# Window attention on one core: VectorE's exp in four passes instead of five, a larger share of score tiles for GpSimd, and a padded lead-in

## The chip, the cores and the metric

The kernel runs on one core of one Trainium2 chip. The metric is the device time of one execution in microseconds (us). Before the change it was 1091.46 us, the median of 3 runs (1091.45 to 1091.47).

Five engines matter here. In this kernel TensorE (PE in the profile) multiplies matrices into PSUM. ScalarE (ACT), VectorE (DVE) and GpSimd (POOL) compute element by element, and SyncE (SP) starts transfers. The other tiles that this text names are in SBUF. Each row of the profile carries a line number of the kernel file.

## The reference, cut to what matters

```
x: 1 x 224 x 224 x 96, bf16; wqkv: 96 x 288; wo: 96 x 96; stripes 8 wide
qkv = x @ wqkv; q, k, v have 96 channels each
channels 0..47:  28 horizontal stripes of 8 x 224 = 1792 tokens
channels 48..95: 28 vertical stripes of 224 x 8 = 1792 tokens
each stripe: softmax(q @ k.T / sqrt(48)) @ v
out = concat(horizontal, vertical) @ wo
```

Two stripes are handled together as one pair, so there are 28 pairs. The 1792 x 1792 scores of the two stripes of a pair are cut into 49 tiles of 128 x 1024. That makes 28 x 49 = 1372 score tiles, and each needs one exp of 131,072 elements. Getting those exponentials done is most of the work that is not on TensorE.

Of the kernel before, what the change touches and what calls it, by code (L numbers as in the profile page):

```python
# [11 lines left out]
ALU = mybir.AluOpType  # L12
# [8 lines left out]
def bass_standalone__window_attn_cswin__vision_kernel(  # L21
# [25 lines left out]
    NGTOT = NP * NG  # L47
# [3 lines left out]
    VS = 10  # L51
    NXB = 3
    NTMP = 5
    NZP = 1
    PCH = NTOK // 4
    PU = PCH // SW
    NBD = 3
    SWITCH = 100.0
    DPOL = 0
    SLACK = 120  # L60
    PACE = 1
    FDUE = 20.0
    DSLACK = 120.0
    GRP = 2
    NBA = 8
    LOOK = 8
    NPT = 400
    XPV = 3
    NBP = 3
    NRES = 0  # L70
    RDUE = 0
    KWP = 1
    KWL = 0
    HOLD = 0.0
    HOLD2 = 0
    DUEO = 18
    DUES = 2
    DUE1 = 0
    DUEV = 10
    LATE = 10  # L80
    UTH = 3
    PSPAN = 12
    SAFE = 100
    WGAP = 170
    ORD = 1
    LOOKP = 32
    WARM = 600
    NCHT = NP * NCH
    KA = C2 + 1
    KD = C2 + 2  # L90
# [11 lines left out]
    with es:  # L102
# [104 lines left out]
        def t_ps(n):  # L207
            return 1.0417 * n + 75.0
# [91 lines left out]
        rr = [0]  # L300
# [9 lines left out]
        def fill_bank():  # L310
            if startup[0]:
                rr[0] += 1
                return 4 + rr[0] % 4
            if tail[0]:
                bs = sorted((4, 5, 6, 7), key=lambda i: vis(bank_free[i]) if bank_free[i] != "busy" else 1e18)
                return bs[0]
            bi = pvb.get(pv_cur[0])
            if bi is not None:
                return 13 - bi

            return max((6, 7), key=lambda i: 1e18 if bank_free[i] == "busy" else vis(bank_free[i]))
# [419 lines left out]
        def pick_pe():  # L741
# [47 lines left out]
            if D["cur"] is None and fits(240.0, "r64", DSLACK):  # L789
                G = max(progress(), lastA[0]) + LOOK  # L790
                while G < NGTOT and taken[G] is not None:
                    G += 1
                if G < NGTOT - 6:
                    deps = tile_deps(G)
                    if deps is not None:
                        ws = list(deps) + [D.get("free")]
                        if all(vis(w) <= t for w in ws):
                            taken[G] = "d"
                            ev = plan_QK(G, 4, KD, ws)
                            D["cur"] = dict(G=G, k=0, prev=ev, qk=ev)  # L800
                            return True
# [94 lines left out]
            return True  # L896

        dps = ps[:, 4 * 512:6 * 512]
        D_OCC = [t_ps(1024), 0.521 * 1024 + 75, 0.26 * 1024 + 75, 0.521 * 1024 + 75, t_ps(1024)]

        def d_step(k, sl):
            if k == 0:
                return lambda e: e.tensor_scalar(tt_sb[:], dps.bitcast(U16)[:, 0:2048:2], CS / 65536.0, CS * CA3, ALU.mult, ALU.add)  # L903
            if k == 1:
                return lambda e: e.tensor_tensor(sq_sb[:], tt_sb[:], tt_sb[:], ALU.mult)  # L905
            if k == 2:
                return lambda e: e.tensor_scalar(sq_sb[:], sq_sb[:], CB, None, ALU.add)  # L907
            if k == 3:
                return lambda e: e.tensor_tensor(tt_sb[:], sq_sb[:], tt_sb[:], ALU.mult)  # L909
            return lambda e: e.scalar_tensor_tensor(PTD[sl][:].bitcast(U16), dps, CC, tt_sb[:], ALU.add, ALU.add)  # L910

        def pick_dve():
            t = now[0]
            if evac_pv:
                chg, bi, P, c, e_pv = evac_pv[0]
                if vis(e_pv) <= t:
                    evac_pv.pop(0)
                    q0, qs = CH_Q0[c], CH_SIZES[c]
                    b = P % 2
                    segs = [(0, qs, OT_sb[b][:, q0:q0 + qs], bank(bi)[:, 0:qs])]  # L920
                    if P == 0:

                        segs = []
                        dst4 = OT_sb[b][:].rearrange("p (bc r dw) -> p r bc dw", r=SW, dw=8)
                        o = q0
                        while o < q0 + qs:
                            r, col = divmod(o, W)
                            nr = (q0 + qs - o) // W if col == 0 else 0
                            n = nr * W if nr else min(W - col, q0 + qs - o)
                            sp = bank(bi)[:, o - q0:o - q0 + n]  # L930
                            if nr:
                                segs.append((o - q0, n, dst4[:, r:r + nr, :, :], sp.rearrange("p (r bc dw) -> p r bc dw", r=nr, dw=8)))
                            else:
                                segs.append((o - q0, n, dst4[:, r, col // 8:(col + n) // 8, :], sp.rearrange("p (bc dw) -> p bc dw", dw=8)))
                            o += n
                    for _, n, dst, sp in segs:
                        ev = add("dve", [e_pv], lambda e, dst=dst, sp=sp: e.tensor_copy(dst, sp), t_ps(n), t_ps(n) + 150.0)  # L937
                    bank_free[bi] = ev
                    ot_ev[chg] = ev
                    return True  # L940
            d = D["cur"]
            if DPOL == 1 and d is not None and d["k"] == 4 and do_d(t):
                return True
            if DPOL == 2 and d is not None and d["k"] >= 3 and do_d(t):
                return True
            if DPOL == 3 and d is not None and (d["k"] == 4 or d["k"] == 0) and do_d(t):
                return True
            if DPOL == 4 and d is not None and do_d(t):
                return True
            if DPOL == 5 and d is not None and d["k"] in (1, 2, 3) and do_d(t):  # L950
                return True
            if DPOL == 6 and d is not None and d["k"] in (1, 2, 3, 4) and do_d(t):
                return True
            for f in evac_q:
                if f.steps[f.k].get("eng", "dve") == "dve" and f.step_ready():
                    if f.do_step():
                        evac_q.remove(f)
                    return True
            if HOLD and d is not None and d["k"] in (0, 4) and not tail[0]:
                for f in evac_q:  # L960
                    if f.k > 0 and f.steps[f.k].get("eng", "dve") == "dve" and f.step_soon(HOLD):
                        return False
                if HOLD2 and pv_cur[0] < NCHT and pv_cur[0] not in pvb and evac_pv and vis(evac_pv[0][4]) <= t + HOLD2:
                    return False
            return do_d(t)
# [21 lines left out]
        def safe(dur):  # L987

            t = now[0]
            d = D["cur"]  # L990
            until = max(tfree["dve"], t)
            if d is None or "p" in d or d["k"] == 0:
                until += D_OCC[0]
            elif d["k"] == 4:
                until += D_OCC[4] + D_OCC[0]
            return t + dur <= until + SAFE

        def pick_pool():
# [51 lines left out]
        def do_d(t):  # L1050
            d = D["cur"]
            if d is not None and "p" in d:
# [5 lines left out]
                D["cur"] = None  # L1058
                pow_q.append(dict(G=d["G"], zi=zi, st=[0, 0], ev=[ev, ev], sl=None))
                return True  # L1060
            if d is not None and d["k"] in (1, 2, 3) and tfree["pool"] > t + 50.0:
                return False
            if d is not None and vis(d["prev"]) <= t:
                sl = D["n"] % NBD
                ws = [d["prev"]]
                ok = True
                if d["k"] == 4:
                    if D["n"] >= NBD:
                        if bufD_ev[sl] is None or vis(bufD_ev[sl]) > t:
                            ok = False  # L1070
                        ws.append(bufD_ev[sl])
                    ws.append(d["qk"])
                if ok:
# [1 line left out]
                    ev = add("dve", ws, d_step(k, sl), D_OCC[k], D_OCC[k] + 107.0)  # L1075
                    d["prev"] = ev
                    d["k"] += 1
                    if k == 4:
                        pe_t = (ev[0], ev[1], ev[2] + 28.0)
                        pt_ev[d["G"]] = (pe_t, PTD[sl], ("d", sl))  # L1080
                        bufD_ev[sl] = None
# [7 lines left out]
        pf0 = prep_fills(0, first=True)  # L1089
        def pad(n):  # L1090
            for _ in range(n):
                add("pe", [e_warm], lambda e: e.matmul(bank(3)[:, :], lhsT=warm[:, 0:128], rhs=warm[:, :], start=True, stop=True), 216.0)

        pf0["K"][0].run_now()
        pf0["Q"][0].run_now()
# [1 line left out]
        for G in range(2):  # L1097
# [2 lines left out]
            qA.append((G, plan_QK(G, 2 * G, KA, tile_deps(G))))  # L1100
            if G == 0:
                pad(0)
        for f in [pf0["K"][1], pf0["V"][0]]:
            f.run_now()

        now[0] = max(vis(ev) for _, ev in qA)
        pick_act()
        now[0] = 0.0

        def early_qk(G):  # L1110
            taken[G] = "a"
            lastA[0] = G
            qA.append((G, plan_QK(G, 2 * (G % 2), KA, tile_deps(G) + [actA[G - 2]])))
        early_qk(2)
        for f in [pf0["V"][1], pf0["K"][2]]:
            f.run_now()
        now[0] = tfree["act"]
        pick_act()
        now[0] = 0.0
        early_qk(3)  # L1120
        for f in [pf0["V"][2], pf0["K"][3]]:
            f.run_now()
        startup[0] = False
        add("dve", [bank_free[4], bank_free[5]], lambda e: e.memset(scr[:, 0:1], 0.0), 60.0)
        D["free"] = (s_dve, cnt["dve"], tfree["dve"] + 60.0)
# [173 lines left out]
```

## The kernel before: the parts that the change touches

The kernel file is a small scheduler. It keeps a model of when each engine becomes free, and from this model it decides, while the program is built, in which order each engine gets its instructions and which engine gets which score tile. The order is then fixed. If an instruction takes longer on the chip than the model thinks, nothing is rearranged, and what waits for it is late. This matters for the whole of this study.

A score tile goes to one of three engines. ScalarE has a true exp. VectorE builds the bits of a bf16 number directly: a cubic in the low 16 bits of the fp32 score corrects the score, and the integer that results is the bit pattern of the exponential. GpSimd does the same in six passes, after VectorE has copied the tile from PSUM to SBUF for it (`zp_sb`).

VectorE's five passes (`dps` is the tile in PSUM, all other operands are in SBUF) and the durations that the model gives them (the means in the profile of before were 1221, 716, 432, 696 and 1219 ns):

```python
D_OCC = [t_ps(1024), 0.521 * 1024 + 75, 0.26 * 1024 + 75, 0.521 * 1024 + 75, t_ps(1024)]

def d_step(k, sl):
    if k == 0:
        return lambda e: e.tensor_scalar(tt_sb[:], dps.bitcast(U16)[:, 0:2048:2], CS / 65536.0, CS * CA3, ALU.mult, ALU.add)
    if k == 1:
        return lambda e: e.tensor_tensor(sq_sb[:], tt_sb[:], tt_sb[:], ALU.mult)
    if k == 2:
        return lambda e: e.tensor_scalar(sq_sb[:], sq_sb[:], CB, None, ALU.add)
    if k == 3:
        return lambda e: e.tensor_tensor(tt_sb[:], sq_sb[:], tt_sb[:], ALU.mult)
    return lambda e: e.scalar_tensor_tensor(PTD[sl][:].bitcast(U16), dps, CC, tt_sb[:], ALU.add, ALU.add)
```

The scheduler is built on the assumption that some passes of VectorE and the instructions of GpSimd hold each other up. The recorded texts call what they contend for "the port"; the traces show only which instructions get longer, not what is behind it. In the trace of before, the square (L905) took 675 to 695 ns where no GpSimd instruction ran during it (126 cases) and up to 1121 where one did (32), the addition behind it (L907) 410 to 429 (143) and up to 724 (15), and the last pass (L910), which reads PSUM and one SBUF tile, 1194 to 1226 with one and 1204 to 1225 without (an overlap under 20 ns is not counted). The scheduler treats passes 1, 2 and 3 as passes to be kept apart from GpSimd's work. It does not start one of them while its model says that GpSimd is busy, and it lets GpSimd start an instruction only if that instruction ends before the next such pass can begin:

```python
def safe(dur):                       # may GpSimd start something that lasts dur?
    ...
    until = max(tfree["dve"], t)
    if d is None or "p" in d or d["k"] == 0:
        until += D_OCC[0]
    elif d["k"] == 4:
        until += D_OCC[4] + D_OCC[0]
    return t + dur <= until + SAFE
...
    if d is not None and d["k"] in (1, 2, 3) and tfree["pool"] > t + 50.0:   # in do_d: VectorE waits
        return False
```

One further pass of VectorE works on SBUF alone all through the kernel and is held back by no such rule (there are also a sum of one column per pair, and the last three final additions). It runs once per pair, 28 times in all, and shifts a part of K. In the trace of before it took 317 to 353 ns in the 23 cases without a GpSimd instruction during it, and 946 to 972 in the 5 with one:

```python
def ev2(e, bk):
    return e.tensor_scalar(KT_sb[b][:, q0:q0 + qs], KT_sb[b][:, q0:q0 + qs], shift[b][:, 0:1], None, ALU.add)
```

## Time and profile before

| | before |
|---|---|
| time | 1091.46 us |
| tiles on ScalarE / VectorE / GpSimd | 1169 / 158 / 45 |
| busy ScalarE / VectorE / GpSimd | 1077.2 / 1047.4 / 584.6 us |
| ScalarE's idle ahead of its tiles | 5.9 us |
| mean granted TensorE clock | 0.993 |

All rows but the first are from the profiled run, and that run took 1096.08 us, 4.6 us more than the median. Of the 28 runs of this kernel in the rounds of the experiments, 14 show a mean clock of 0.999 and took 1091.24 to 1092.15 us, as the median run did. The profiled run spent 13.7 us near its start at half clock, which alone takes 0.6% off the mean clock. So the runs at 0.999 did not have this dip.

The prediction below shows and reads the groups and the stages. Two more lines of the page are needed for the comparison: the granted TensorE clock in 40 equal slices (a digit is tenths of full speed, 9 is 90% or more), and the chain of work that ended last, by engine.

```profile
PEclk7999999999999999999999999999999999999999
...
ACT 71%; DVE 21%; PE 4%; POOL 1%; issue 1%; DMA 0%; SPq 0%; DVEq 0%; POOLq 0%
```

The clock is at 90% or more except in the first slice, and 71% of the last chain are ScalarE's. That is what a kernel bound by ScalarE looks like.

### The profile page before, as it was taken

How to read it: one execution, taken by the hardware profiler on the slowest of the kernel's cores; microseconds unless marked ns; L12 is line 12 of the kernel's file. 1: busy time of each engine (PE TensorE's matmuls, PEld its weight loads, DVE VectorE, ACT ScalarE, POOL GpSimd, SP SyncE). 2: the span in 40 equal slices, each digit the busy share in tenths (PEclk: the TensorE clock that was granted, in tenths of full speed). 3: DMA queues.
4: the chain of work that ended last, by engine and by line, in shares of the span. 5: the costliest groups of instructions: out<-in, count | busy, mean ns of one | idle time of the engine just before them, and what ended most of it. 6: DMA issues, size and time to landing. Idle time of an engine off the chain costs nothing.

```text
span 1094.3 us, 28704 instructions
## 1 busy us (share of the span) xinstructions
PE 1040.7 (95%) x12104; PEld 372.7 (34%) x12104; DVE 1047.4 (96%) x1712; ACT 1077.2 (98%) x1172; POOL 584.6 (53%) x451
## 2 busy tenths in 40 slices
PE   9999999999999999999999999999999999999997
PEld 2333333332333333233333333333333333333332
DVE  5999999999999999999999999999999999999996
ACT  6999999999999999999999999999999999999997
POOL 0544555453545645364564465656565565656563
PEclk7999999999999999999999999999999999999999
DMA  5301001101110120110111122122222222221111
GB/s 99 69 9 35 19 18 36 36 10 27 36 27 10 35 36 7 30 35 17 20 35 27 35 44 41 39 41 42 41 41 40 39 42 41 39 41 38 24 28 37
DMA packets 169001, 37.37 MB, mean 34 GB/s; under 512 B 168872, under 2 KB 168872, under 8 KB 168872
## 3 DMA queue, kind: packets, MB, share of 16 engines
q1 hardware_dynamic: 167256, 35.35, 17.3%
q8 instruction: 94, 1.54, 0.6%
q10 hardware_dynamic: 1616, 0.18, 0.1%
q14 instruction: 35, 0.29, 0.1%
HBM read 0.15 MB, written 9.63 MB: 9 GB/s over the span
## 4 chain that ended last, share of the span: by engine, by line
ACT 71%; DVE 21%; PE 4%; POOL 1%; issue 1%; DMA 0%; SPq 0%; DVEq 0%; POOLq 0%
ACT PTA L892 71%; DVE tt_sb L903 4%; DVE PTD L910 3%; DVE sq_sb L905 2%; DVE tt_sb L909 2%; PE ps L194 2%; PE ps L853 1%; DVE sq_sb L907 1%; DVE KT_sb L522 1%; DVE zp_sb L1056 1%; DVE tmp L624 1%; DVE OT_sb L937 1%; DVE V_sb L431 1%; POOL PTP L985 1%; DVE QT_sb L498 1%
## 5 line engine op out<-in xcount | busy, mean ns | idle before, releaser
L892 ACT ACTIVATE PTA<-ps 128x1024 bf16<-128x1024 f32 x1169 | 1075.0, 1214 | 5.9 <-PE ps L194 5.1
L194 PE MATMUL ps<-QT_sb,KT_sb 49*64 49x512 bf16 (+3 forms) x5488 | 486.5, 369 | 38.9 <-ACT PTA L892 25.5
L853 PE MATMUL ps<-PTA,V_sb 128*64 128x512 bf16 (+1 forms) x2674 | 422.9, 367 | 0.6 <-DVE Ph_sb L584 0.2
L190 PEld LDWEIGHTS <-KT_sb 49*64 49x64 bf16 (+1 forms) x5488 | 137.4, 103 | 335.0 <-issue 321.9
L903 DVE TENSOR_SCALAR tt_sb<-ps 128x1024 f16<-128x1024 uint16 x158 | 192.9, 1221 | 11.6 <-PE ps L194 7.1
L910 DVE SCALAR_TENSOR_TENSOR PTD<-ps,tt_sb 128x1024 uint16<-128x1024 f32 x158 | 192.5, 1219 | 1.3
L853 PEld LDWEIGHTS ps<-PTA,V_sb 128*64 128x64 bf16 x2674 | 119.8, 108 | 204.1 <-issue 162.8
L647 POOL TENSOR_TENSOR out_sb<-tmp,Ph_sb 128x480 bf16<-128x480 f32 (+2 forms) x89 | 105.6, 1195 | 110.9 <-DVE sq_sb L907 57.9
L978 POOL TENSOR_TENSOR uq_sb<-up_sb 128x1024 f16<-128x1024 f16 (+1 forms) x52 | 101.3, 1952 | 111.6 <-DVE sq_sb L907 57.5
L982 POOL TENSOR_TENSOR up_sb<-uq_sb,up_sb 128x512 f16<-128x512 f16 (+1 forms) x65 | 112.3, 1732 | 84.8 <-DVE sq_sb L907 27.4
L984 POOL TENSOR_TENSOR zp_sb<-zp_sb,up_sb 128x512 f32<-128x512 f32 (+1 forms) x74 | 111.2, 1508 | 54.6 <-DVE sq_sb L907 31.7
L976 POOL TENSOR_SCALAR up_sb<-zp_sb 128x1024 f16<-128x1024 uint16 x45 | 47.1, 1047 | 130.3 <-DVE zp_sb L1056 115.4
L905 DVE TENSOR_TENSOR sq_sb<-tt_sb 128x1024 f16<-128x1024 f16 x158 | 113.1, 716 | 0.1
L909 DVE TENSOR_TENSOR tt_sb<-sq_sb,tt_sb 128x1024 f16<-128x1024 f16 x158 | 109.9, 696 | 2.9
L462 PE MATMUL ps<-xT_sb,w_sb 128*64 128x448 bf16 (+3 forms) x448 | 85.7, 380 | 6.1 <-DVE KT_sb L522 3.0
L937 DVE CAST OT_sb<-ps 128x512 bf16<-128x512 f32 (+5 forms) x118 | 69.3, 591 | 1.4 <-PE ps L853 1.4
L907 DVE TENSOR_SCALAR sq_sb<-sq_sb 128x1024 f16<-128x1024 f16 x158 | 68.2, 432 | 2.2
L1056 DVE COPY zp_sb<-ps 128x1024 f32<-128x1024 f32 x45 | 55.0, 1222 | 8.8 <-POOL PTP L985 4.6
L853 PE MATMUL ps<-PTD,V_sb 128*64 128x512 bf16 (+1 forms) x360 | 62.1, 362 | 0.0
L985 POOL TENSOR_SCALAR PTP<-zp_sb 128x512 uint16<-128x512 f32 (+1 forms) x66 | 57.4, 870 | 5.7 <-POOL zp_sb L984 0.2
L624 DVE TENSOR_TENSOR tmp<-ps,rc 128x480 f32<-128x480 f32 (+2 forms) x92 | 53.2, 578 | 1.1
L522 DVE TENSOR_TENSOR KT_sb<-ps,shift 128x448 bf16<-128x448 f32 (+2 forms) x84 | 51.6, 615 | 2.1 <-PE ps L462 2.1
(55 smaller groups left out, 668.3 us busy)
## 6 DMA issues: line engine op xcount, KB each, us to landing
out_dram<-out_sb SPq DMA_DIRECT2D x389, 24.0 KB, 1.9
xT_sb<-in_x_dram SPq DMA_TRANSPOSE x332, 2.6
w_sb<-in_wqkv_dram ACTq DMA_DIRECT2D x2, 54.0 KB, 3.1
out_dram<-out_sb ACTq DMA_DIRECT2D x3, 24.0 KB, 1.9
wo_sb<-in_wo_dram SPq DMA_DIRECT2D x4, 9.0 KB
wo_sb<-one_sb SPq DMA_DIRECT2D x4, 0.0 KB
```

The source lines that it names most:

```text
L190: return e.add_instruction(mybir.InstLdweights(tile_size=(64, 64), tile_position=pos, name=nc.get_next_instruction_name(), engine=mybir.En ...
L194: return e.add_instruction(mybir.InstMatmult(start_tensor_calc=True, stop_tensor_calc=True, tile_size=(64, 64), tile_position=pos, ldweigh ...
L647: return e.tensor_tensor(out_sb[b][:, wdw, k0:k0 + n, :], tmpi[:, 0:n, :], Ph_sb[:, k0:k0 + n, j, :], ALU.add)
L853: ins = e.matmul(bk[64 * wdw:64 * wdw + 64, 0:qs], lhsT=V_sb[b][:, wdw, kt, :], rhs=pt[:, wdw * 512 + i * qs:wdw * 512 + (i + 1) * qs], st ...
L892: e = add("act", [ev, bufA_ev[sl]], lambda e, base=base, sl=sl: e.activation(PTA[sl][:], ps[:, base * 512:(base + 2) * 512], ACTF.Exp, sca ...
L903: return lambda e: e.tensor_scalar(tt_sb[:], dps.bitcast(U16)[:, 0:2048:2], CS / 65536.0, CS * CA3, ALU.mult, ALU.add)
L905: return lambda e: e.tensor_tensor(sq_sb[:], tt_sb[:], tt_sb[:], ALU.mult)
L909: return lambda e: e.tensor_tensor(tt_sb[:], sq_sb[:], tt_sb[:], ALU.mult)
L910: return lambda e: e.scalar_tensor_tensor(PTD[sl][:].bitcast(U16), dps, CC, tt_sb[:], ALU.add, ALU.add)
L978: return e.tensor_tensor(q, u, u, ALU.mult)
L982: return e.tensor_tensor(u, q, u, ALU.mult)
L984: return e.tensor_tensor(z, z, u, ALU.add)
```

## The change

The intent is to give VectorE's exp one pass fewer, and to leave only one pass of it, the square, that the scheduler keeps apart from GpSimd's work. GpSimd then has more room, gets 77 tiles instead of 45, and ScalarE and VectorE get fewer. A second `zp_sb` buffer lets VectorE copy the next tile while GpSimd still works on the last. Padding matmuls in the first microseconds should keep the TensorE clock up. The core of the diff, with cuts marked by `...`:

```diff
-    NZP = 1
+    NZP = 2
-    DPOL = 0
+    DPOL = 5
...            (12 more settings of the scheduler: GRP, LOOK, NBP, HOLD, DUEO, DUEV, WARM and others)
-        D_OCC = [t_ps(1024), 0.521 * 1024 + 75, 0.26 * 1024 + 75, 0.521 * 1024 + 75, t_ps(1024)]
+        D_OCC = [t_ps(1024), 0.521 * 1024 + 75, 1.0417 * 1024 + 65, t_ps(1024)]
...
             if k == 2:
-                return lambda e: e.tensor_scalar(sq_sb[:], sq_sb[:], CB, None, ALU.add)
-            if k == 3:
-                return lambda e: e.tensor_tensor(tt_sb[:], sq_sb[:], tt_sb[:], ALU.mult)
+                return lambda e: e.scalar_tensor_tensor(tt_sb[:], sq_sb[:], CB, tt_sb[:], ALU.add, ALU.mult)
...
-            elif d["k"] == 4:
-                until += D_OCC[4] + D_OCC[0]
+            elif d["k"] == 2:
+                until += D_OCC[2] + D_OCC[3] + D_OCC[0]
+            elif d["k"] == 3:
+                until += D_OCC[3] + D_OCC[0]
...
-            if d is not None and d["k"] in (1, 2, 3) and tfree["pool"] > t + 50.0:
+            if d is not None and d["k"] == 1 and tfree["pool"] > t + 50.0:
                 return False
...
+        pad(PADA)                    # 5 padding matmuls
         early_qk(2)
+        for f in [pf0["K"][1], pf0["V"][0]]:
+            f.run_now()
+        early_qk(3)
...            (single pads between the next fills; the fifth score tile is started early too)
```

The new pass has two SBUF inputs, `sq_sb` and `tt_sb`, and the new rules let GpSimd run beside it.

Some passages are cut out of the prediction and of three expectations (e1_psum_operand, e8_delay, e16_five_kshift), because no trace of this case shows what they say: general statements on the engines, ahead of and behind the example of L909, and what rested on them. The forecast's sum has lost no term: 8.4 + 1064.0 + 2.0 + 6.1 = 1080.5 us of span, less 2.8 = 1077.7, all from the profile and the times of before. Cut is one of the two heavy rivals, that the new pass is slow in itself, with its size; the chance of 0.18 still counts it. Cut is also the second argument against the port rival. What the trace shows of it is that L905 and L909 take 0.72 and 0.70 us where the new pass was counted at 1.22. So no exp pass that reads SBUF alone and takes 1.22 us had been seen beside GpSimd. That the old pass L907 excludes GpSimd is the order's own assumption; the trace has the few longer cases given above.

> **What bounds the kernel now.** I read the page's table of busy time first, then the groups of instructions, then the busy time by stage, then the timeline of GpSimd and VectorE around one of VectorE's passes.
>
> ```profile
> PE 1040.7 (95%) x12104; PEld 372.7 (34%) x12104; DVE 1047.4 (96%) x1712; ACT 1077.2 (98%) x1172; POOL 584.6 (53%) x451
> ```
>
> Three engines look full. PE's share is no limit by itself, because matmul ends are modelled. The groups (count, busy us, mean ns, idle before) say which engine sets the pace:
>
> ```profile
> L892 ACT ACTIVATE PTA<-ps 128x1024 bf16<-128x1024 f32 x1169 | 1075.0, 1214 | 5.9 <-PE ps L194 5.1
> L903 DVE TENSOR_SCALAR tt_sb<-ps 128x1024 f16<-128x1024 uint16 x158 | 192.9, 1221 | 11.6 <-PE ps L194 7.1
> L910 DVE SCALAR_TENSOR_TENSOR PTD<-ps,tt_sb 128x1024 uint16<-128x1024 f32 x158 | 192.5, 1219 | 1.3
> ...
> L905 DVE TENSOR_TENSOR sq_sb<-tt_sb 128x1024 f16<-128x1024 f16 x158 | 113.1, 716 | 0.1
> L909 DVE TENSOR_TENSOR tt_sb<-sq_sb,tt_sb 128x1024 f16<-128x1024 f16 x158 | 109.9, 696 | 2.9
> ...
> L907 DVE TENSOR_SCALAR sq_sb<-sq_sb 128x1024 f16<-128x1024 f16 x158 | 68.2, 432 | 2.2
> L1056 DVE COPY zp_sb<-ps 128x1024 f32<-128x1024 f32 x45 | 55.0, 1222 | 8.8 <-POOL PTP L985 4.6
> ```
>
> There are 1169 + 158 + 45 = 1372 score tiles (28 window pairs of 49). ScalarE takes 1169, VectorE 158 in five passes, GpSimd 45 behind a VectorE copy. ScalarE's activations overlap (mean 1214 ns), so its cost per tile is 1075.0 / 1169 = 0.9196 us, and it idles 5.9 us in all. So ScalarE is the bound, and a tile taken from it is worth 0.92 us. By stage (busy us of PE, PEld, DVE, ACT, POOL, then granted clock):
>
> ```profile
> 8.40:10.00 1.60, 0.67 (x12) 0.30 (x9) 0.05 (x1) 1.60 (x2) 0.00 (x0) 1.00 0.76 139
> 10.00:15.00 5.00, 5.00 (x56) 1.82 (x53) 4.00 (x8) 4.06 (x5) 0.00 (x0) 0.61 0.45 85
> 15.00:20.00 5.00, 5.00 (x32) 1.07 (x30) 2.43 (x4) 3.34 (x4) 0.00 (x0) 0.50 0.44 82
> 20.00:25.00 5.00, 5.00 (x28) 1.01 (x28) 3.86 (x8) 3.66 (x4) 0.00 (x0) 0.53 0.45 82
> 25.00:30.00 5.00, 5.00 (x56) 1.57 (x54) 4.23 (x7) 4.94 (x6) 2.09 (x2) 1.00 0.43 81
> 30.00:1080.00 1050.00, 1004.52 (x11795) 360.38 (x11797) 1023.46 (x1650) 1049.17 (x1144) 577.57 (x434) 1.00 0.17 32
> ```
>
> ScalarE's first tile starts at 8.40 us and its last ends at 1088.24. Between 10 and 30 us it loses 0.94 + 1.66 + 1.34 + 0.06 = 4.0 us, just where the clock has fallen to 0.5; in the next 1050 us it loses 0.8. The span is then lead 8.40 + work 1075.0 + idle 4.8 + tail 6.1 = 1094.3.
>
> [...]L909, a tensor_tensor with two SBUF inputs:
>
> ```profile
> 607.36 1.60 POOL L647 TENSOR_TENSOR out_sb<-tmp,Ph_sb 128x480 bf16<-128x480 f32 x1 [8.12 <-DVE sq_sb L907]
> 609.91 1.09 POOL L647 TENSOR_TENSOR out_sb<-tmp,Ph_sb 128x480 bf16<-128x480 f32 x1 [0.94 <-DVE tmp L624]
> ...
> 607.31 0.69 DVE L909 TENSOR_TENSOR tt_sb<-sq_sb,tt_sb 128x1024 f16<-128x1024 f16 x1
> ...
> 608.04 1.22 DVE L910 SCALAR_TENSOR_TENSOR PTD<-ps,tt_sb 128x1024 uint16<-128x1024 f32 x1
> ```
>
> The same GpSimd addition takes 1.09 us alone and 1.60 when it starts 0.05 us after L909: 0.51 longer, most of the 0.64 that L909 still had to run. L910, with one SBUF input, ran beside GpSimd at its usual 1.22. [...]
>
> **The change part by part.** Counts are those of the built program.
>
> *VectorE's exp.* The multiply-add pair L907 and L909 becomes one scalar_tensor_tensor on sq_sb and tt_sb. Removed per tile: 432 + 696 = 1128 ns. Added: one pass, which I take at 1.22 us as L910 [...]. So the arithmetic is no cheaper, by about 0.09 us; the gain, if any, is in the port. Before, three passes per tile held it, 0.69 + 0.42 + 0.69 us by their medians; the change holds GpSimd back for the square alone (0.69). VectorE now runs 138 tiles and 77 copies: 138 x (1.221 + 0.716 + 1.22 + 1.219) = 604, 77 x 1.222 = 94, and all else 1047.4 - 676.6 - 55.0 = 316; sum 1014 us, against 1047 before. Over a span of some 1080 that is 94%: still tight, a little looser than now.
>
> *GpSimd.* It takes 77 tiles, 32 more, with two zp buffers so that a copy need not wait for the tile before. Unblocked durations in the timeline are 1.05 us for one-input passes (0.62 for a half), 1.89 to 2.12 for two-input ones (1.03 to 1.15 for a half). By the program's counts of whole and half passes this gives 741 us for 77 tiles (9.6 each) plus 86 for the final additions: 827 us. The square passes take 138 x 0.69 = 95 us and the shifted-K passes about 12 of port time. Together 934 of the some 1040 us between the first copy and the last tile, 90%; the same sum before is 519 + 296 = 815, 78%. It fits if the new pass takes no port.
>
> *ScalarE.* It keeps 1372 - 138 - 77 = 1157 tiles: 12 fewer, 12 x 0.9196 = 11.0 us off the path that sets the end. Its work is 1157 x 0.9196 = 1064.0.
>
> *Lead-in.* Five padding matmuls go between the second and third score tile, where PE now waits 0.93 us for a DMA at 9.5 us, and single ones later; the third and fourth tiles move ahead of the K and V projections. If the clock stays at 1.00 most of the 4.0 us go; I count 3 saved. The first tile's inputs do not change, so 8.40 stays, and so does the tail of 6.1.
>
> *The rest* (look-ahead, hold and due settings) moves order, not work; the bf16 filler matmuls on a zero operand fall from 262 to 162. I allow 0.2 us more idle.
>
> Sum: 8.4 + 1064.0 + 2.0 idle + 6.1 = 1080.5 of span. The clocked time lies 1094.3 - 1091.46 = 2.8 below the profiled span, so 1077.7, I say **1078**: 1.2% less.
>
> **The rivals.** *The new pass takes the port after all.* For: [...] L909 shows that two SBUF inputs exclude GpSimd, and the order now lets GpSimd run beside that pass. Against: the author's whole order rests on one port pass[...]. Cost: 138 x 1.22 = 168 us more of port, 934 + 168 = 1102 in a window of 1040. GpSimd or VectorE then sets the pace, at 1140 us at the least, more likely 1150 to 1250. [...] *A milder one:* GpSimd at 90% falls behind in the stretches with many final additions; VectorE's copies wait for zp, and ScalarE for tiles: 5 to 20 us lost, 1083 to 1098. *The lead-in's clock falls anyway:* 1080 to 1081. *The other way:* 2% faster means 1069.6, which needs 8 us more than my sum; ScalarE's work alone with the same lead and tail, and no idle at all, is 1075.7 after the 2.8. I see no source for it.
>
> **Range and chances.** The two heavy rivals get about 0.18 together, since the change is re-tuned throughout, which speaks for a pass that was tried. The milder ones widen the upper side: 1070 to 1096. Faster by over 2%: 0.03; within 2%: 0.79; slower by over 2%: 0.18.
>
> **What would show it.** Right: 1157 activations, about 0.92 us each, idle under 3 us; L911 near 1.22 us, with GpSimd passes beside it at their unblocked durations; GpSimd 80% busy or so; granted clock 1.00 between 10 and 25 us. Wrong: L911 well over 1.22 or GpSimd passes behind it longer by over 0.5 us (port); [...] long waits of the zp copy for GpSimd (supply); ScalarE waiting for score matmuls at a clock of 0.5 (lead-in).

## The result, and the profile after

| | before | after |
|---|---|---|
| time, median of 4 | 1091.47 us (1091.45 to 1094.61) | 1255.95 us (1240.72 to 1261.87) |
| tiles on ScalarE / VectorE / GpSimd | 1169 / 158 / 45 | 1157 / 138 / 77 |
| ScalarE's idle ahead of its tiles | 5.9 us | 129.6 us |
| mean granted clock of the profiled run | 0.993 | 0.922 |

The changed kernel is slower by 14.5%: ratio 1.1452, 95% interval 1.1344 to 1.156. A ratio here and below is the mean time of one kernel's fast runs over the mean time of the other's fast runs of the same rounds, so it is not quite the ratio of the medians. One of the four runs, 1261.87 us, counts as slow (clock 0.897) and is left out of the ratio. The profiled run took 1240.72 us.

The first lines to read on the page of the kernel after are busy time, clock and chain:

```profile
PE 1107.2 (89%) x12012; PEld 381.6 (31%) x12012; DVE 1143.9 (92%) x1507; ACT 1096.0 (88%) x1160; POOL 970.4 (78%) x705
...
PEclk9998879999999789999899898999998799989795
...
DVE 64%; PE 27%; ACT 4%; POOL 3%; issue 2%; DVEq 0%; POOLq 0%
```

ScalarE has fallen from 71% of the last chain to 4%. VectorE is busy for 1143.9 us, though 1014 had been summed for it, and GpSimd for 970.4. And the clock digits show a second thing: dips all along the kernel, where before there was one at the start.

The groups of instructions (count, then busy us and mean ns of one, then idle before and what ended it) show where VectorE's time went:

```profile
L895 ACT ACTIVATE PTA<-ps 128x1024 bf16<-128x1024 f32 x1157 | 1093.9, 1054 | 129.6 <-PE ps L197 103.4
...
L911 DVE SCALAR_TENSOR_TENSOR tt_sb<-sq_sb,tt_sb 128x1024 f16<-128x1024 f16 x138 | 267.8, 1940 | 2.2
...
L907 DVE TENSOR_SCALAR tt_sb<-ps 128x1024 f16<-128x1024 uint16 x138 | 168.5, 1221 | 23.4 <-PE ps L197 17.9
L912 DVE SCALAR_TENSOR_TENSOR PTD<-ps,tt_sb 128x1024 uint16<-128x1024 f32 x138 | 167.2, 1211 | 0.1
...
L1060 DVE COPY zp_sb<-ps 128x1024 f32<-128x1024 f32 x77 | 93.9, 1220 | 12.5 <-PE ps L197 6.0
L909 DVE TENSOR_TENSOR sq_sb<-tt_sb 128x1024 f16<-128x1024 f16 x138 | 103.7, 751 | 0.1
```

L911 is the new pass: 1940 ns on average. L912 is the same operation with one of its inputs in PSUM, and takes 1211. The view of the tile `tt_sb` adds the spread (minimum, median and maximum in ns, then the time of the first and the last):

```profile
L911 DVE SCALAR_TENSOR_TENSOR tt_sb<-sq_sb,tt_sb x138: 1206/1945/3125, 18.6 to 1218.6; 128x1024 f16<-128x1024 f16 x138
```

At its best the pass takes 1206 ns, about the 1.22 us that were counted. So the operation is not slow in itself. Something delays it by anything between 0 and 1.9 us. The timeline (start us, length us, engine) shows one case:

```profile
604.21 2.24 POOL L980 TENSOR_TENSOR uq_sb<-up_sb 128x1024 f16<-128x1024 f16 x1 [2.17 <-DVE rc L583]
...
604.99 2.55 DVE L911 SCALAR_TENSOR_TENSOR tt_sb<-sq_sb,tt_sb 128x1024 f16<-128x1024 f16 x1
...
607.67 0.66 DVE L587 TENSOR_TENSOR Ph_sb<-ps,rc 128x480 bf16<-128x480 f32 x1
...
608.39 0.58 PE L427 MATMUL ps<-w_sb,xT_sb 96*128 96x48 bf16 x10 [1.40 <-DVE Ph_sb L587]
...
609.58 1.02 ACT L895 ACTIVATE PTA<-ps 128x1024 bf16<-128x1024 f32 x1 [1.50 <-PE ps L197]
```

GpSimd's square ends at 604.21 + 2.24 = 606.45. L911 was started at 604.99, while it ran, and ends at 607.54, which is 1.09 us after GpSimd's end. A pass at its best takes 1.21 us, so it looks as if this one did almost all of its work once GpSimd was through. It is the common case: 125 of the 138 passes started while a GpSimd instruction ran. They took 1219 to 3125 ns, 1950 by the median, and 124 of them ended after that instruction did, by 1082 ns by the median. The other 13 took 1206 to 1225. L587 came behind it on VectorE, and TensorE waited 1.40 us for L587. ScalarE then waited 1.50 us for TensorE. The windows around it (busy us of PE, PEld, DVE, ACT and POOL, then the clock) show what followed:

```profile
600.00:605.00 5.00, 4.76 (x56) 1.43 (x52) 4.50 (x8) 4.82 (x6) 2.75 (x3) 1.00 0.00 0
605.00:610.00 5.00, 3.52 (x46) 1.50 (x42) 4.96 (x6) 3.50 (x5) 3.67 (x4) 0.82 0.01 3
610.00:615.00 5.00, 5.00 (x46) 1.37 (x42) 2.41 (x4) 3.43 (x4) 2.58 (x2) 0.50 0.00 0
615.00:620.00 5.00, 5.00 (x80) 2.34 (x80) 4.73 (x9) 4.69 (x6) 2.93 (x3) 1.00 0.14 26
```

TensorE's wait shows as 3.52 busy of 5.00. The clock then halves, and in the next five microseconds ScalarE is busy for only 3.43 of 5.00. One blocked pass has thus been paid for twice: by the wait, and by the slow matmuls after it.

How often this happens can be counted. The trace records the granted clock as stretches with a start and a length. Take the time from ScalarE's first tile to the end of its last one, split it into full and halved clock, and subtract 0.9196 us for each tile that ended in either part:

| profiled run | halved clock: stretches, us | lost at halved clock | lost at full clock |
|---|---|---|---|
| before | 1, 14 | 4.5 us | 0.4 us |
| after | 27, 189 | 85 us | 73 us |

The changed kernel loses about as much at full clock, where delays make tiles late, as in 27 stretches of halved clock. The first is 0.070 us for each of the 1044 tiles that ended at full clock, and the second is 113 tiles at 1.67 us each in place of 0.92. Which delay started which stretch is not told by this split; the cases looked at in the timeline are like the one above.

The lead-in did what it was meant to. These windows answer to those of the same stages in the prediction:

```profile
10.00:15.00 5.00, 4.87 (x63) 2.05 (x62) 3.67 (x8) 4.29 (x6) 0.00 (x0) 1.00 0.45 94
15.00:20.00 5.00, 4.91 (x49) 1.49 (x46) 4.29 (x7) 5.00 (x6) 0.00 (x0) 1.00 0.33 70
20.00:25.00 5.00, 4.33 (x46) 1.23 (x42) 4.82 (x9) 5.00 (x7) 0.00 (x0) 1.00 0.43 89
```

The clock stays at 1.00, and ScalarE idles 0.7 us in these 15 us, where it had lost 3.9 in the profiled run of before. Half of the runs of before did not have the dip, so against the median there was little here to gain.

### The profile page after: what moved, and what is told of

Same layout as the page of the kernel before. It is cut to its first block, busy times and chain, and to the rows that moved or that the text cites. A ratio compares the mean times of both kernels' runs of the same rounds, so it can differ in the third digit from the quotient of the medians.

```text
span 1238.7 us, 28720 instructions
## 1 busy us (share of the span) xinstructions
PE 1107.2 (89%) x12012; PEld 381.6 (31%) x12012; DVE 1143.9 (92%) x1507; ACT 1096.0 (88%) x1160; POOL 970.4 (78%) x705
## 4 chain that ended last, share of the span: by engine, by line
DVE 64%; PE 27%; ACT 4%; POOL 3%; issue 2%; DVEq 0%; POOLq 0%
DVE tt_sb L911 17%; PE ps L197 12%; DVE tt_sb L907 10%; PE ps L856 10%; DVE PTD L912 6%; DVE sq_sb L909 6%; DVE zp_sb L1060 4%; DVE OT_sb L939 4%; ACT PTA L895 4%; DVE tmp L627 2%; DVE V_sb L434 2%; DVE KT_sb L525 2%; DVE Ph_sb L587 2%; PE ps L465 2%; DVE QT_sb L497 2%; DVE QT_sb L501 2%
## 5 line engine op out<-in xcount | busy, mean ns | idle before, releaser
L895 ACT ACTIVATE PTA<-ps 128x1024 bf16<-128x1024 f32 x1157 | 1093.9, 1054 | 129.6 <-PE ps L197 103.4
L197 PE MATMUL ps<-QT_sb,KT_sb 49*64 49x512 bf16 (+3 forms) x5488 | 525.1, 396 | 41.3 <-ACT PTA L895 16.1
L911 DVE SCALAR_TENSOR_TENSOR tt_sb<-sq_sb,tt_sb 128x1024 f16<-128x1024 f16 x138 | 267.8, 1940 | 2.2
L986 POOL TENSOR_TENSOR zp_sb<-zp_sb,up_sb 128x512 f32<-128x512 f32 (+1 forms) x107 | 202.4, 1898 | 38.7 <-DVE KT_sb L525 8.2
L984 POOL TENSOR_TENSOR up_sb<-uq_sb,up_sb 128x512 f16<-128x512 f16 (+1 forms) x119 | 190.2, 1606 | 21.8 <-DVE V_sb L434 7.0
L980 POOL TENSOR_TENSOR uq_sb<-up_sb 128x512 f16<-128x512 f16 (+1 forms) x122 | 171.7, 1414 | 44.0 <-DVE rc L583 11.1
L907 DVE TENSOR_SCALAR tt_sb<-ps 128x1024 f16<-128x1024 uint16 x138 | 168.5, 1221 | 23.4 <-PE ps L197 17.9
L912 DVE SCALAR_TENSOR_TENSOR PTD<-ps,tt_sb 128x1024 uint16<-128x1024 f32 x138 | 167.2, 1211 | 0.1
L978 POOL TENSOR_SCALAR up_sb<-zp_sb 128x1024 f16<-128x1024 uint16 (+1 forms) x88 | 92.7, 1055 | 89.0 <-DVE zp_sb L1060 41.6
L650 POOL TENSOR_TENSOR out_sb<-tmp,Ph_sb 128x480 bf16<-128x480 f32 (+2 forms) x88 | 106.5, 1215 | 22.9 <-DVE rc L621 9.1
L987 POOL TENSOR_SCALAR PTP<-zp_sb 128x1024 uint16<-128x1024 f32 (+1 forms) x85 | 107.1, 1260 | 18.9 <-DVE tt_sb L911 6.4
L982 POOL TENSOR_SCALAR uq_sb<-uq_sb 128x1024 f16<-128x1024 f16 (+1 forms) x87 | 101.7, 1169 | 25.2 <-DVE tt_sb L911 6.2
L1060 DVE COPY zp_sb<-ps 128x1024 f32<-128x1024 f32 x77 | 93.9, 1220 | 12.5 <-PE ps L197 6.0
L909 DVE TENSOR_TENSOR sq_sb<-tt_sb 128x1024 f16<-128x1024 f16 x138 | 103.7, 751 | 0.1
L727 PE MATMUL ps<-QT_sb,KT_sb 49*64 49x256 bf16 (+1 forms) x784 | 57.5, 289 | 0.0
```

The lines of the kernel that those rows point to most:

```text
L197: return e.add_instruction(mybir.InstMatmult(start_tensor_calc=True, stop_tensor_calc=True, tile_size=(64, 64), tile_position=pos, ldweigh ...
L895: e = add("act", [ev, bufA_ev[sl]], lambda e, base=base, sl=sl: e.activation(PTA[sl][:], ps[:, base * 512:(base + 2) * 512], ACTF.Exp, sca ...
L911: return lambda e: e.scalar_tensor_tensor(tt_sb[:], sq_sb[:], CB, tt_sb[:], ALU.add, ALU.mult)
L980: return e.tensor_tensor(q, u, u, ALU.mult)
L984: return e.tensor_tensor(u, q, u, ALU.mult)
L986: return e.tensor_tensor(z, z, u, ALU.add)
```

## The experiments

Theory P (the port theory of the recorded texts): the new pass, which reads two SBUF operands, and GpSimd's instructions hold each other up, and the order lets them run at the same time. Rival H: the operation itself is slow on two fp16 operands from SBUF, whatever GpSimd does. Rival S: the new order, with 77 tiles on GpSimd and its new settings, is too tight whatever the pass does. Each run below was measured beside the kernel before on the same chip. Twelve kernels ran. In the expectations, e1_psum_operand (or e1) is the run with the new pass reading PSUM, e10_kshift (or e10) the one with the shift of K in its accumulator form as well, and e2_five the one with the five passes of before. The 2.8 us that several of them subtract are answered in the part on the prediction. Times are the median and the range of four runs; ratios are those of fast runs, with a 95% interval, and a run in the slow state is named.

### The same order, with the new pass reading PSUM

```diff
-  e.scalar_tensor_tensor(tt_sb[:], sq_sb[:], CB, tt_sb[:], ALU.add, ALU.mult)
+  e.scalar_tensor_tensor(tt_sb[:], dps, 0.0, tt_sb[:], ALU.mult, ALU.add)
```

This gives a wrong result on purpose. Instruction order, waits and size stay; only one of the two SBUF inputs is gone.

> The changed kernel, same order on every engine, but the new pass reads its first operand from PSUM in place of sq_sb, so it has one SBUF input (wrong result on purpose, same length of pass). Port theory (the pass with two SBUF inputs excludes GpSimd): all passes at 1.21 to 1.23 us, GpSimd's at their unblocked durations, ScalarE idle under 8 us, clock near 0.99, total 1072 to 1090 us. Rival (the re-tuned order, with 77 GpSimd tiles, is too dense whatever the port does): total stays above 1200 us. [...]

The time was 1096.51 us (1091.62 to 1099.11), ratio 1.0017 [0.998, 1.0053]. The groups of this run:

```profile
L895 ACT ACTIVATE PTA<-ps 128x1024 bf16<-128x1024 f32 x1157 | 1064.8, 1202 | 13.3 <-PE ps L197 12.9
...
L911 DVE SCALAR_TENSOR_TENSOR tt_sb<-ps,tt_sb 128x1024 f16<-128x1024 f32 x138 | 168.1, 1218 | 2.2
```

One operand's place is worth some 160 us. The pass is back at 1218 ns and nearly all the loss is gone, though GpSimd still has its 77 tiles and the order is the same. That is theory P, and rival S can at most explain what is left. The time lies a little above the expected 1072 to 1090. The trace has four stretches of halved clock left, and each begins within 5 us of a shift of K that took 1.1 to 1.95 us in place of 0.33. Eight other shifts were lengthened to over 1.1 us without a fall, so a lengthened one does not always bring one. One of the four, with the windows around it:

```profile
588.18 1.89 POOL L980 TENSOR_TENSOR uq_sb<-up_sb 128x1024 f16<-128x1024 f16 x1
...
588.25 1.95 DVE L516 TENSOR_SCALAR KT_sb<-KT_sb,shift 128x448 bf16<-128x448 bf16 x1
```

```profile
585.00:590.00 5.00, 4.69 (x69) 2.27 (x71) 4.93 (x8) 5.00 (x7) 4.92 (x4) 1.00 0.21 40
590.00:595.00 5.00, 3.24 (x30) 0.69 (x22) 4.09 (x7) 3.47 (x4) 3.31 (x4) 0.77 0.24 46
```

The shift started 0.07 us after GpSimd's square and ended 0.13 us after it. It is a second unguarded pass, and it has always been in the kernel.

### The same, with the shift of K in its accumulator form as well

```diff
-  e.tensor_scalar(KT_sb.., KT_sb.., shift[b][:, 0:1], None, ALU.add)
+  e.tensor_scalar(KT_sb.., KT_sb.., shift[b][:, 0:1], None, ALU.add, ALU.add, accum_out=junk[:, 0:1])
```

The edit is on top of the one before. This form also writes an accumulator. Whether it gets longer beside GpSimd, as the plain form does, is what the run asks.

> As e1_psum_operand (port-free new pass, wrong result on purpose, same order), and the in-place shift of K, the other VectorE pass that the order does not guard, written in a form with an accumulator output. In e1 that pass took up to 1.95 us beside GpSimd, and each of four stretches of halved clock began behind one. Theory (those collisions are the remaining loss): K passes all near 0.55 us, clock 1.00 throughout, ScalarE idle under 5 us, total 1077 to 1086 us. Rival (the 77-tile order is simply too dense for the chip): as e1, 1092 to 1099 us.

The time was 1082.99 us (1082.56 to 1084.03), ratio 0.9903 [0.9868, 0.9938]. The shift took 673 to 745 ns in all 28 cases, so it never got longer as the plain form had in e1 (up to 1950). At 679 ns by the median (0.55 us had been expected, an estimate) it costs twice as much as the plain form's 0.33 without GpSimd, and a read of the accumulator, 83 ns, comes on top. The clock never halved after the first tile, and ScalarE hardly idled:

```profile
L897 ACT ACTIVATE PTA<-ps 128x1024 bf16<-128x1024 f32 x1157 | 1063.3, 1174 | 3.3 <-PE ps L198 2.7
```

This is the time that the prediction had expected of the change, within some 5 us, and it is what rival S must be measured by: the new order itself is fine if nothing blocks. GpSimd is busy for 871.6 us here, where the blocked passes had made it 970.4. So VectorE's passes and GpSimd's both got longer where they met.

### The change with only the shift of K in its accumulator form

> The changed kernel, correct result, with only the shift of K taken off the port (accumulator form); the new exp pass keeps its two SBUF inputs. If the exp pass is the main loss and the K shift a small one: 1235 to 1256 us against 1256. If the K shift's collisions set off most of the clock falls: 1180 us or less.

The time was 1256.92 us (1237.22 to 1259.17). Only one of its four runs counts as fast, 1237.22 us; the other three are slow, so there is no verdict. Beside the changed kernel's 1240.72 to 1258.76 it buys nothing that can be measured. L911 has a mean of 1947 ns (the profiled run is a slow one). As far as these runs can tell, the small cause shows only once the large one is gone.

### The pass without GpSimd beside it

```diff
-    NPT = 400
+    NPT = 0        # no tile for GpSimd
```

> The changed kernel, correct result, its new pass untouched (two SBUF inputs), with no score tiles on GpSimd (only the final additions stay there). Order: 1205 ScalarE, 167 VectorE tiles. Port theory: with GpSimd mostly idle the pass runs at 1.22 to 1.32 us mean; 8.3 + 1205 x 0.9196 + 2 + 6.1 - 2.8 = 1122 us (1115 to 1140). Rival (the pass is slow whatever GpSimd does): mean of 1.9 us, above 1220 us.

The time was 1124.74 us (1123.4 to 1126.26), ratio 1.0292, with 1205 tiles on ScalarE. The new pass, untouched, with its two SBUF inputs:

```profile
L911 DVE SCALAR_TENSOR_TENSOR tt_sb<-sq_sb,tt_sb 128x1024 f16<-128x1024 f16 x167 | 204.6, 1225 | 3.2
```

Rival H is out: without GpSimd's tiles the pass takes what L912, with its operand from PSUM, takes in the same run (1215 ns by the median). The time is what 1205 x 0.92 us plus lead and tail come to, and it shows what GpSimd's 77 tiles were to save.

### Does VectorE's lengthening alone explain the loss?

A blocked pass does two things: it lengthens VectorE's work, and the delay falls unevenly, by 0 to 1.9 us. This run has the lengthening only. The kernel with the PSUM operand gets a copy of 620 columns from PSUM, planned at 0.72 us, ahead of each new pass.

```diff
+  e.tensor_copy(scr2[:, 0:620], dps[:, 0:620])     # ahead of pass k = 2
   e.scalar_tensor_tensor(tt_sb[:], dps, 0.0, tt_sb[:], ALU.mult, ALU.add)
```

> As e1_psum_operand, with a VectorE copy of 620 PSUM columns (0.72 us, one PSUM input[...]) before each new pass: VectorE is lengthened by what the passes lost in the changed kernel on average, without any port conflict. VectorE's sum becomes about 1041 + 99 = 1140 us. If only the lengthening of VectorE (with the clock falls that follow) makes the loss: 1225 to 1260 us as in the changed kernel. If the scatter of the blocked passes and GpSimd's own delays matter as well: 1150 to 1210 us.

The time was 1213.34 us (1199.06 to 1217.56), ratio 1.105 [1.0964, 1.1135]. One run, 1217.56 us, counts as slow. The time fell between the two expectations, with one fast run in the lower one. The copy took 797 ns by the mean, and VectorE was busy for 1137.7 us, against 1143.9 after the change. The same split of the loss as above says why:

| profiled run | halved clock: stretches, us | lost at halved clock | lost at full clock |
|---|---|---|---|
| PSUM operand | 4, 14 | 7 us | 6 us |
| PSUM operand with even delay | 12, 143 | 58 us | 77 us |
| after | 27, 189 | 85 us | 73 us |

At full clock the even delay costs as much as the real one (77 and 73 us). So a longer VectorE queue is enough for that part, without uneven delays or a blocked GpSimd. The real change has 27 halved stretches for 12, and loses 27 us more in them. Its delays are uneven, and GpSimd's passes are delayed as well (its last addition, on `zp_sb`, takes 1898 ns by the mean, and 1682 with the even delay). Which of the two adds those stretches is not separated.

### The four passes alone, in the kernel before

> The kernel before with the four-pass exp alone, as the change schedules it; order comes out with 1161 / 164 / 47 tiles. Port theory: the new pass mean 1.5 to 1.9 us, clock below 0.99, total 1130 to 1200 us though GpSimd has only 47 tiles. Rival (77 tiles and two copies are what overloads): 1161 tiles x 0.9196 + 8.4 + 4.8 + 6.1 - 2.8 = 1084 us.

The time was 1303.74 us (1299.96 to 1306.62), ratio 1.1914, worse than the whole change. The sign was expected, the size was not (1130 to 1200). The group of the new pass here:

```profile
L908 DVE SCALAR_TENSOR_TENSOR tt_sb<-sq_sb,tt_sb 128x1024 f16<-128x1024 f16 x164 | 297.5, 1814 | 3.0
```

There are 164 such passes instead of 138. The loss at full clock is 57 us, but 328 us of the run lie at halved clock, in 41 stretches, and they lose 159 us. So the pass harms this order too, with only 47 tiles on GpSimd, and the harm differs by what the clock does. Why this order falls more often than the re-tuned one is not separated.

### The changed order with the five passes of before

```diff
-  D_OCC = [.., 1.0417 * 1024 + 65, t_ps(1024)]               # 4 passes, square guarded
+  D_OCC = [.., 0.26 * 1024 + 75, 0.521 * 1024 + 75, t_ps(1024)]  # 5 passes, 1 to 3 guarded
```

> The changed kernel with the old five passes, GpSimd held back for three of them; all else of the change kept. The order comes out with 1161 ScalarE, 147 VectorE and 64 GpSimd tiles. Port theory: no long passes, 8.4 + 1161 x 0.9196 + 2 idle + 6.1 - 2.8 = 1081 us (1076 to 1090). Rival (the order's new settings or the two copies in flight are to blame): above 1150 us.

The time was 1124.31 us (1119.93 to 1127.34), ratio 1.0273 [1.0238, 1.0308]: missed. Seven stretches of halved clock lost 16 us, and 26 us were lost at full clock. Several stretches followed a lengthened shift of K (0.87 to 1.96 us), so that was tried apart, with the accumulator form in this kernel:

> The changed kernel with the five passes of before (as in e2_five, 1124.31 us) and the shift of K in its accumulator form[...]. In e2_five four of the seven groups of cold stretches follow, within some microseconds, a shift of K that took 0.87 to 1.96 us in place of 0.33. Theory A, that the unguarded shift of K is what started them: the granted clock is 0.995 or more and the time 1085 to 1098 us. Rival B, that the five guarded passes and the tight re-tuned order do it by themselves: the clock stays below 0.99 and the time is 1108 to 1125 us. In between: both have a part. The shift itself should take 0.68 us, as in e10_kshift.

The time was 1114.4 us (1111.55 to 1118.99), ratio 1.0185 [1.0143, 1.0228]. The halved stretches fall from 7 to 3 and their loss from 16 to 4.5 us, but the loss at full clock stays at 26. One of its runs had a mean clock of 1.000 and still took 1111.55. So most of it is rival B of this expectation, though the clock, 0.990 to 1.000, is above what B had named: with 64 tiles and three guarded passes, the order itself is slow. The page suggests where: in four of GpSimd's groups, 118 us of idle end with the second of the guarded passes, so GpSimd is held back while they run. That was not tested. If it is so, the change's idea, fewer passes for which GpSimd is held back, has something to gain.

### The order told the truth about the pass

```diff
-  if d is not None and d["k"] == 1 and tfree["pool"] > t + 50.0:
+  if d is not None and d["k"] in (1, 2) and tfree["pool"] > t + 50.0:
...        (and `safe` as in the kernel before: no GpSimd instruction may reach into pass 2)
```

> The changed kernel, correct result, with the order told that the new pass takes the port: GpSimd is held back for it as for the square. Order: 1163 ScalarE, 147 VectorE, 62 GpSimd tiles. Port theory: passes at 1.22 to 1.35 us mean, GpSimd's durations behind it longer by what is left of it; total 1085 to 1130 us, no better than the five passes (1124). Rival (a two-SBUF pass is slow by itself in this place): 1200 us or more.

The pass came back to a mean of 1283 ns, as expected, but the time was 1176.09 us (1170.13 to 1186.01), ratio 1.0769, and the expected 1085 to 1130 was missed. It lost 53 us at halved clock and 36 at full clock. The guards rest on modelled durations: the square, guarded too, took 812 ns by the mean here, and the unguarded shift of K a median of 894. Holding both engines back for a pass of 1.2 us is not a way to pay for it.

### The lead-in alone

> The kernel before with the lead-in of the change alone (padding matmuls, two tiles moved up, fill banks); 1171 ScalarE tiles, 2 more. Both theories: clock 1.00 from 10 to 25 us, idle 3 us less, 2 x 0.92 us more work: 1089 to 1091 us. If the padding delays the first tiles: 1092 or more.

The time was 1114.23 us (1112.03 to 1121.35), ratio 1.0205 [1.0162, 1.0249]: missed. The padding worked: ScalarE was busy 23.22 us of the first 30, and 19.78 before. But the scheduler derives the whole order anew from any edit (tiles 1171 / 161 / 40), and this order has five later stretches of halved clock, which lose 17 us; at full clock it loses 2. No pass was blocked ahead of the first one, at 130 us. TensorE was only a little thin there, and why was not looked into:

```profile
125.00:130.00 5.00, 3.88 (x60) 1.82 (x60) 4.94 (x9) 5.00 (x7) 2.11 (x2) 1.00 0.01 3
130.00:135.00 5.00, 3.92 (x39) 1.35 (x35) 4.36 (x8) 3.15 (x4) 2.40 (x3) 0.56 0.00 0
```

An edit that changes this order at all can cost 20 us without doing anything wrong. The same can lie in the times of the five-pass kernels, of the four passes alone and of the order told the truth, which were derived anew as well.

### Are the pads what keeps the clock?

The kernel with nothing blocked, but its eight lead-in pads cut from 512 to 16 columns. The order stays the same.

> As e10_kshift, same order, but the eight padding matmuls of the lead-in are cut from 512 to 16 columns, which takes away their work and keeps everything else (the four that the kernel before had too stay). If the padding is what keeps the clock up: clock near 0.5 in part of 10 to 25 us, 2 to 4 us more than e10 (1083.0), so 1085 to 1087. If moving two tiles up is what helps: no difference, 1082.5 to 1083.5.

The time was 1085.56 us (1083.63 to 1089.64), ratio 0.9938 [0.9905, 0.9971], against 0.9903 [0.9868, 0.9938] with the pads: the intervals overlap. The mean clocks do not: 0.989 to 0.996 in the four runs with tiny pads, 0.998 to 0.999 with whole ones. The windows of the profiled runs show where. First with tiny pads, then with whole ones:

```profile
15.00:20.00 5.00, 5.00 (x36) 1.12 (x32) 2.70 (x4) 3.99 (x5) 0.00 (x0) 0.67 0.40 73
```

```profile
15.00:20.00 5.00, 4.78 (x48) 1.31 (x44) 3.91 (x6) 5.00 (x6) 0.00 (x0) 1.00 0.39 73
```

So the moved tiles alone do not keep the clock, and the pads do. From 10 to 20 us ScalarE is busy 4.13 + 3.99 us with tiny pads and 4.29 + 5.00 with whole ones: 1.2 us lost.

### A version in which every exp pass reads PSUM

The cubic can be written as three factors, (f + s1)(f + s2) t, with f the low 16 bits of the score. Each pass then reads f from PSUM and one tile from SBUF (now fp32). The shift of K has its accumulator form, GpSimd is not held back at all, and the scheduler's settings were searched anew in its model. The result is correct.

```diff
+  lo16 = dps.bitcast(U16)[:, 0:2048:2];  RT = (-CB) ** 0.5;  UN = 65536.0 / CS
-  k == 1: e.tensor_tensor(sq_sb[:], tt_sb[:], tt_sb[:], ALU.mult)
-  k == 2: e.scalar_tensor_tensor(tt_sb[:], sq_sb[:], CB, tt_sb[:], ALU.add, ALU.mult)
+  k == 1: e.scalar_tensor_tensor(sq_sb[:], lo16, (CS * CA3 - RT) * UN, tt_sb[:], ALU.add, ALU.mult)
+  k == 2: e.scalar_tensor_tensor(tt_sb[:], lo16, (CS * CA3 + RT) * UN, sq_sb[:], ALU.add, ALU.mult)
```

> A candidate, correct result: the cubic as three factors, each new one read from PSUM, so that all four VectorE passes have at most one SBUF input (fp32 tiles between), the shift of K in its accumulator form, GpSimd not held back at all, order re-tuned: 1160 ScalarE, 117 VectorE, 95 GpSimd tiles. Port theory: no VectorE pass above 1.25 us, GpSimd at its unblocked durations, 8.3 + 1160 x 0.9196 + 2 + 6.1 - 2.8 = 1080 us (1076 to 1090). If a pass with a PSUM and an SBUF input conflicts after all: above 1120 us.

The time was 1081.0 us (1080.69 to 1081.28), ratio 0.9883 [0.9848, 0.9918]: 1.2% less than before, which is under the 2% from which a verdict says faster, but clear of noise. It is the best correct version of this study. Tiles are 1160 / 117 / 95.

```profile
L897 ACT ACTIVATE PTA<-ps 128x1024 bf16<-128x1024 f32 x1160 | 1063.7, 1281 | 2.1 <-PE ps L198 2.1
...
L916 DVE SCALAR_TENSOR_TENSOR tt_sb<-ps,sq_sb 128x1024 f32<-128x1024 uint16 x117 | 142.1, 1214 | 0.2
```

The square at 0.72 us has become a pass of 1.215, so VectorE does fewer tiles. But no exp pass took more than 1226 ns, with GpSimd busy for 958.9 of the 1035 us from 30 us on, and no stretch at halved clock follows the first tile.

### How little idle time halves the clock

Halved stretches occur in the profiled runs of before and after and in most of the experiments; there are none behind the first tile in the kernel with the PSUM operand and the other form of the shift, and none in the version in which every exp pass reads PSUM. In the traces of before and after, all 28 stretches begin on a grid of 3.413 us and are one to nine such steps long (most are one or two). The windows of five experiments fit: behind 30 us their time at halved clock is 13.6, 34.1, 37.5, 123.0 and 143.4 us (PSUM operand, lead-in alone, five passes, order told the truth, even delay), which is 4, 10, 11, 36 and 42 steps.

TensorE's busy share (as the profile models it) in the one grid step ahead of each fall can therefore be compared with the steps that no fall followed. In the profiled run after, behind the lead-in, all 12 full-clock steps with a share below 0.55 were followed by a fall; the 27 falls followed shares of 0.33 to 0.68, and the lowest share that no fall followed is 0.56. The kernel before has no such step below 0.78, and no fall there. A wait of 1.2 to 1.5 us is more than a third of a step. It leaves a share of 0.56 to 0.65, where both occurred in the run after, so it can be enough. What brings the clock back is not shown: in the kernel before, TensorE was busy all through the four steps at half clock (3.41 us of each), and the clock was full again only after the fourth.

## Why the prediction was wrong

**The bound now, and ScalarE's count: right.** ScalarE had 1157 tiles at 0.92 us. Where nothing blocks, its idle is 3.3 us and the span 1080.8 us, for a sum of 1080.5. That the two agree so closely is partly luck: the first tile starts at 9.09 us there, not at 8.40.

**From span to time: wrong by 4.6 us.** The 2.8 us were the span of one run, 1094.3, less the median of other runs, 1091.46. The profiled run itself took 1096.08, so its time lies 1.8 above its span, as in the kernel with nothing blocked (1082.56 and 1080.8). The sum was therefore 1082.3, not 1077.7, and 1082.99 is what was measured where nothing blocks. This does not touch the step that failed.

**The lead-in: right for the profiled run.** The clock stayed at 1.00 and 3.2 us were saved between 10 and 25 us, for 3 predicted. But the runs of before at the median's time had not lost them, as their clock of 0.999 shows.

**VectorE's sum: too small.** With nothing blocked VectorE was busy for 1036.5 us, not 1014. Its exp passes and copies come to 697 us, as summed (698). The error is in "all else 316", which was taken as VectorE's busy time less the exp groups: instructions overlap by some 96 us there, and by 81 with fewer passes. The shift of K in its accumulator form adds the rest. GpSimd's 827 us measured 871.6. Both still fitted.

**A pass slow in itself: did not come true.** The pass takes 1206 ns at its best and 1225 by the mean without GpSimd's tiles.

**The step that failed** is in GpSimd's part: "It fits if the new pass takes no port." The pass and GpSimd's instructions do hold each other up. It was taken at 1.22 us "as L910", and L910 has one SBUF input where the new pass has two. It measured 1.94, which is 138 x 0.72 = 99 us more on VectorE. L909 in the trace of before, with two SBUF inputs, had shown it: a GpSimd addition beside it took 1.60 us in place of 1.09. The prediction named this as its first rival and put it aside, mainly because "the change is re-tuned throughout, which speaks for a pass that was tried". That was an argument about the author, set against one about the operands, and it was wrong: the settings came from a model in which the pass and GpSimd do not meet.

**The rival's own size.** "1140 us at the least, more likely 1150 to 1250" came from adding up the time of the passes that exclude GpSimd. The measured time is just above this, and one of the two halves of the loss was not in the sum at all. In the profiled run 73 us were lost at full clock, and 85 more in the 27 stretches in which the TensorE clock was halved; both all but go once the pass reads PSUM (6 and 7 us). The prediction looked at the clock in the lead-in only.

**The shift of K** was counted as "about 12 us of port time". As time that is right. As a trigger it was missed: once the new pass reads PSUM, the blocked shifts alone go with four halvings and 1096.51 instead of 1082.99 us.

What stays open: why the kernel with the four passes alone falls to the halved clock so much more often than the full change, and which single waits make the five-pass order lose 26 us at full clock.

## What to carry to other kernels

Before believing a pass-count saving on VectorE, count its SBUF operands: here a pass that reads two tiles from SBUF took 1.94 us by the mean with GpSimd's tiles and 1.22 without, and moving one operand to PSUM was worth some 160 us, where the whole change had been expected to save 13. In a fixed order, look for every pass that gets longer beside GpSimd and that no rule guards, however short: here the shift of K, 0.33 us without GpSimd and up to 1.95 beside it, delays what is behind it. And watch the granted TensorE clock all through the kernel: here falls followed steps of 3.4 us in which TensorE was 0.33 to 0.68 busy, and the 113 tiles that ended at halved clock cost 1.67 us each in place of 0.92.
